# Moving the third output block's operand loads ahead of the gate loads, and giving the last four tiles four separate PSUM buffers

## The chip, the core and the metric

The kernel runs on one NeuronCore of a Trainium2 chip, as one launch. The metric is the device time of that launch in microseconds. Five engines work side by side, each through its own list of instructions in order: TensorE (PE, with the weight load shown apart as PEld), VectorE (DVE), ScalarE (ACT), GpSimd (POOL) and SyncE (SP, which here only starts DMAs). An instruction that waits for a semaphore holds up everything behind it on the same engine.

## The reference

For one sequence of S = 2048 tokens with D = 512 features, F = 1792 and 32 heads of 16:

```
xn = layernorm(x)
s  = softmax(q k^T / 4) v @ wo          with q, k, v = xn @ wqkv, 32 heads
g  = silu((silu(xn @ w_gate) * (xn @ w_up)) @ w_down)
out = x + s * g
```

Everything is float32. The kernel splits each operand of the large products into a high part, rounded to the matmul's reduced float32, and the low remainder, and adds three products (high by high, high by low, low by high).

## The kernel before

**Stages.** A prologue normalises x, transposes it and projects q, k and v, which go to DRAM. Then comes the main loop: 32 attention units (8 groups of four heads by 4 query blocks of 512 tokens), each of 8 steps. A step on TensorE is a fixed row of work: four score products (L809), the four products with v of the step before (`values`, L356) with ScalarE's exponentials (L811) between, four more score products, and then a share of side work.

**The side work** is a queue of generators, in order: four passes of the feed-forward net, a first part of the output projection of the last block, and `project_out(0)`, `project_out(1)`, `project_out(2)`, the output projections of query blocks 0, 1 and 2. `fill` takes products from it, `plan` has set how many per step. For the projections a share is one tile of 128 tokens: 12 pairs of products, each pair writing `bankx` and `banky` (`both`, L174). There are twelve such tiles; they take the last steps of unit 30 and all eight steps of unit 31. When a tile's last pair is done, VectorE empties the two banks into `y` (L328, L329), GpSimd multiplies by the gate and adds x (`store_out`, L313, L314) and the result is stored (L315). The next tile's first pair writes the same two banks, so TensorE waits for L328 and L329 of the tile before.

**Operands of an output block.** `load_out(b, c)` (L278, SP queue) brings part c of the attention output of block b from DRAM (`o_d`) into a raw slot, and `split_o` (L261 a cast, L262 a subtraction, VectorE) makes the high and low operand from it. Blocks 0 and 2 live in the tile `hh`, block 1 in `wd`; block 2 uses block 0's raw slots and operand slots again. A raw slot is free once block 0's split has read it, an operand slot once block 0's last product has. Part 3 of block 2 is not loaded: `finish(30)` makes it from the attention accumulator (L363 to L377, then a split).

**The order around it** is set by `out_steps`, called once per step behind the share. It issues a block's loads when a condition on the queue holds, appends its splits one step later, and hands VectorE at most two splits per step. `load_gates(t)` (L283 the gate, L284 x, SP queue) fetches what tile t needs on GpSimd. It reuses the slots of tile t - 4, so L283 waits for that tile's L313 and L284 for that tile's stored result. `after` is a list of things to do; `catch_up` runs it early in the next step.

**The end.** Behind the loop, block 3's output is finished by hand: `products(t, c)` (L856) for its four tiles into `outs[t]`, which are the four halves of the two score tiles; `normalise` for the last unit in two halves; then per tile `gated` (L863) and `stored` (L869 an addition, L870 the store).

Of the kernel before, what the change touches and what calls it, by code (L numbers as in the profile page):

```python
# [25 lines left out]
NB = 4  # L26
TB = S // NB
NT = TB // P
DT = D // P
# [21 lines left out]
def tile_block(ctx: ExitStack, tc: tile.TileContext, x, wqkv, wo, w_gate, w_up, w_down, out):  # L51
# [22 lines left out]
    banky = pone.tile([P, 512], F32, name="banky")  # L74
    banks = (bankx, banky)
    acc = [pone.tile([P, 512], F32, name=f"acc{i}") for i in range(2)]
# [77 lines left out]
    after = []  # L154

    def catch_up():
        while after:
            after.pop(0)()
# [13 lines left out]
    def both(lhs, rhs, start, stop):  # L172
        for bank, h in zip(banks, halves):
            mm(bank, lhs[h], rhs[h], start=start, stop=stop)  # L174
# [85 lines left out]
    def split_o(dst, src):  # L260
        dve.tensor_copy(dst[0], src)  # L261
        dve.tensor_sub(dst[1], src, dst[0].bitcast(F32))  # L262
# [11 lines left out]
    def load_out(b, c):  # L274
        whole = (hh, wd, hh)[b].rearrange("p f j t -> p (f j) t")
        parts_o[b, c] = whole[:, 2 * DT + c].bitcast(F32)
        lhs[b, c] = whole[:, 2 * c], whole[:, 2 * c + 1]
        sp.dma_start(parts_o[b, c], o_d[c, b])  # L278

    def load_gates(t):  # L280
        gt[t] = (hh, wd)[t % NT // 2].rearrange("p f j t -> p (f j) t")[:, 14 + t % 2].bitcast(F32)
        xr[t] = plain[t % NT]
        sp.dma_start(gt[t], g_d[rows[t]])  # L283
        sp.dma_start(xr[t], x[rows[t]])  # L284

    stage = {}
    ready = [0] * NB
    splits = []

    def out_steps():  # L290
        for b in range(NB - 1):
            if b not in stage and (len(queue) <= (NB, NB, 2)[b] if b != 1 else 0 in stage and now > stage[0]):
                for c in range(DT - 1):
                    load_out(b, c)
                stage[b] = now
            if b in stage and b < 2 and (b, 1) not in stage and now > (u0 + b) * steps:
                load_out(b, DT - 1)
                stage[b, 1] = now
            if b in stage and (b, 2) not in stage and now > stage[b]:
                splits.extend((b, c) for c in range(DT - 1))  # L300
                stage[b, 2] = now
                for t in range(0 if b else NT):
                    load_gates(t)
            if (b, 1) in stage and (b, 5) not in stage and now > stage[b, 1]:
                splits.insert(0 if not b else len(splits), (b, DT - 1))
                stage[b, 5] = now
        for _ in range(min(2, len(splits))):
            b, c = splits.pop(0)
            split_o(lhs[b, c], parts_o[b, c])
            ready[b] += 1  # L310

    def store_out(t, y):
        pool.tensor_mul(y, y, gt[t])  # L313
        pool.tensor_add(xr[t], y, xr[t])  # L314
        (pool if t < end - 1 else sp).dma_start(out[rows[t]], xr[t])  # L315

    def project_out(b, n=DT):
        catch_up()
        for j in range(NT if n == DT else EARLY):
            t = b * NT + j  # L320
            i = 0
            for c in range(n):
                for a, w in ((0, 0), (0, 1), (1, 0)):
                    both(lhs[b, c][a][:, j * P:(j + 1) * P], fx[:, w, c], i == 0, i == 3 * n - 1)
                    i += 1
                    if i == 3 * n and n == DT:
                        y = one.tile([P, D], F32, tag="th", name="y")
                        dve.tensor_scalar(y, bankx, 0.5, None, op0=ALU.mult)  # L328
                        dve.scalar_tensor_tensor(y, banky, 0.5, y, op0=ALU.mult, op1=ALU.add)  # L329
                        store_out(t, y)  # L330
                        if b + 2 < NB:
                            load_gates(t + NT)
                    elif i == 3 * n:
                        dve.tensor_copy(facc[:, j], bankx)
                        dve.tensor_add(facc[:, j], banky, facc[:, j])
                    yield 3 * n - i
# [50 lines left out]
    units = NG * NB  # L387
# [4 lines left out]

    queue = [[None, ffn(b), NF * 3 * (DC + NT)] for b in range(NB)]
    queue += [[None, project_out(NB - 1, DT - 1), EARLY * 3 * (DT - 1)]]
    queue += [[b, project_out(b), NT * 3 * DT] for b in range(NB - 1)]
    total = sum(q[2] for q in queue)
    given = 0

    now = -1
# [46 lines left out]
    with ExitStack() as pro:  # L446
# [294 lines left out]
        with tc.If(fast < 1):  # L741
            with tc.tile_pool(name="gen", bufs=1) as gen:
                for h in range(2):
                    pool.memset(qst[0][h * HALF:h * HALF + 2].bitcast(F32), 0.0)
                for g in range(NG):
                    for b in range(NB):
# [3 lines left out]
                        for j in range(NB):  # L750
                            load_k(g, j, j % 2)
                            for i in range(4 * NT):
                                h, t = divmod(i, NT)
# [28 lines left out]
    score = [spool.tile([P, 2, 512], F32, name=f"score{i}") for i in range(2)]  # L782
# [8 lines left out]
    now = 0  # L791
# [5 lines left out]
    for u in range(units):  # L797
        g, b = divmod(u, NB)
        q = qst[u % 2]
        for kp in range(steps):  # L800
            now = u * steps + kp
# [29 lines left out]
            if g + 1 < NG and (b == 0 and kp == 0 or b == NB - 1 and kp in (2, 4, 6)):  # L831
                load_k(g + 1, kp // 2)
                load_v(g + 1, kp // 2)
            out_steps()
            if now == (units - 1) * steps + 1:
                load_gate()
# [5 lines left out]
    assert not queue and not after and given == total  # L842
    hi = two.tile([P, 2, D], F32R, tag="guh", name="rh")[:, 0]
    lo = one.tile([P, D], F32R, tag="th", name="rl")
    outs = [i[:, n] for i in score for n in range(2)]
    half = TB // 2
    cols = [slice(n * half, (n + 1) * half) for n in range(2)]
    spare, *y = [ppool.tile([P, 2, TB], F32, tag="pr", name="y") for _ in range(3)]
# [13 lines left out]
    def gated(t):  # L862
        dve.scalar_tensor_tensor(y[t], outs[t], 0.5, gate[t], op0=ALU.mult, op1=ALU.mult)  # L863

    def stored(t, parts=1):
        n = D // parts
        for i in range(parts):
            w = slice(i * n, (i + 1) * n)
            dve.tensor_add(y[t][:, w], y[t][:, w], (facc[:, t] if t < EARLY else last[t])[:, w])  # L869
            (sp, nc.scalar)[(t + i) % 2].dma_start(out[rows[(NB - 1) * NT + t], w], y[t][:, w])  # L870
# [17 lines left out]
    for t in (2, 3):  # L888
        products(t, DT - 1)
        gated(t)  # L890
    stored(2)
    stored(3, 2)


_INS = ["A_x", "A_wqkv", "A_wo", "B_w_gate", "B_w_up", "B_w_down"]
# [21 lines left out]
```

## Time and profile before

| what | value |
|---|---|
| median of 3 runs | 1445.43 us (1444.51 to 1446.19) |
| the profiled execution's own time | 1447.62 us |
| its span, first to last instruction | 1445.8 us |
| granted TensorE clock, mean | 0.997 |
| TensorE busy | 1431.7 us (99%) |
| ScalarE busy | 1111.2 us (77%) |
| VectorE busy | 536.5 us (37%) |
| GpSimd busy | 89.1 us (6%) |

The profile comes from one execution. The time of that execution is its span and 1.8 us that lie outside it. Rows of the timeline read: start in us from the span's start, duration, engine, line, operation, output and input; in brackets how long the engine had been idle before and what ended the idle time. Rows of the waits read: who waited for whom, then us in total, how often, and the longest.

### The profile page before, as it was taken

What the parts mean: (1) busy time and instruction counts of PE and PEld (TensorE: products, weight loads), DVE (VectorE), ACT (ScalarE), POOL (GpSimd) and SP (SyncE); (2) the same over time, 40 slices, a digit from 0 to 9 for tenths busy, and PEclk for the clock granted to TensorE, in tenths of its full rate; (3) what the DMA queues carried; (4) which work ended last, traced back from release to release, by engine and by line L of the source; (5) the groups of instructions that cost most, each with busy time, mean ns of one, the idle gap of its engine ahead of it and who ended that gap; (6) DMA issues with size and microseconds to landing.
All of it is one profiled execution on the core that took longest, in us unless ns stands there. A gap on an engine that the chain in (4) does not pass through costs nothing.

```text
span 1445.8 us, 26814 instructions
## 1 busy us (share of the span) xinstructions
PE 1431.7 (99%) x11227; PEld 805.9 (56%) x11227; DVE 536.5 (37%) x900; ACT 1111.2 (77%) x1235; POOL 89.1 (6%) x103
## 2 busy tenths in 40 slices
PE   9999999999999999999999999999999999999988
PEld 7777655555555555555555555555555555555554
DVE  5543344213523443143334341234234421433735
ACT  6733688888888888788888888888888887888753
POOL 4200200000000000000000000000000000000244
PEclk9999999999999999999999999999999999999999
DMA  6778642032264330143534310333644211411553
GB/s 218 264 246 248 157 114 63 21 95 60 68 144 128 84 78 20 43 102 82 118 110 106 94 42 8 87 91 89 140 104 103 63 34 24 104 41 60 194 171 107
DMA packets 127524, 149.15 MB, mean 103 GB/s; under 512 B 12588, under 2 KB 79404, under 8 KB 126628
## 3 DMA queue, kind: packets, MB, share of 16 engines
q1 hardware_dynamic: 122196, 126.84, 34.0%
q0 software_dynamic: 4912, 20.12, 3.7%
q8 instruction: 91, 1.49, 0.4%
q10 hardware_dynamic: 288, 0.39, 0.1%
q14 instruction: 37, 0.30, 0.1%
HBM read 107.20 MB, written 40.11 MB: 102 GB/s over the span
## 4 chain that ended last, share of the span: by engine, by line
PE 96%; issue 1%; POOL 1%; DVE 1%; DMA 1%; ACT 0%; SPq 0%; POOLq 0%; DVEq 0%
PE acc L356 32%; PE bankx L174 30%; PE score L809 20%; PE ps L569 6%; PE banky L174 5%; PE ps L571 3%; PE acc L544 0%; POOL pair L314 0%; PE acc L493 0%; DMA hh<-o_d 0%; PE score L856 0%; PE ps L600 0%; DMA out_dram<-pair 0%; POOL y L313 0%; DMA out_dram<-y 0%
## 5 line engine op out<-in xcount | busy, mean ns | idle before, releaser
L811 ACT ACTIVATE pr<-score 128x1024 f32<-128x1024 f32 x1024 | 993.3, 1023 | 230.1 <-PE score L809 228.3
L356 PE MATMUL acc<-pr,vst 128*17 128x512 f32 x4096 | 489.2, 595 | 0.0
L809 PE MATMUL score<-qst,kst 50*128 50x512 f32 x2048 | 352.7, 421 | 0.9 <-ACT vt L631 0.9
L809 PEld LDWEIGHTS score<-qst,kst 50*128 50x128 f32 x2048 | 177.3, 184 | 264.7 <-ACT pr L811 228.8
L174 PE MATMUL bankx<-fx,guh 64*128 64x512 f32 x896 | 288.6, 392 | 0.0
L174 PE MATMUL banky<-fx,guh 64*128 64x512 f32 x896 | 288.4, 392 | 0.0
L356 PEld LDWEIGHTS acc<-pr,vst 128*17 128x17 f32 x4096 | 93.9, 96 | 234.7 <-issue 233.9
L204 DVE SCALAR_TENSOR_TENSOR ga<-th,bankx 128x512 f32<-128x512 f32 x56 | 38.5, 687 | 446.2 <-ACT th L203 446.2
L174 PEld LDWEIGHTS bankx<-fx,guh 64*128 64x128 f32 x896 | 165.8, 185 | 32.1 <-issue 0.3
L174 PE MATMUL bankx<-fx,gul 64*128 64x512 f32 x448 | 175.3, 391 | 0.0
L174 PE MATMUL banky<-fx,gul 64*128 64x512 f32 x448 | 175.3, 391 | 0.0
L174 PEld LDWEIGHTS banky<-fx,guh 64*128 64x128 f32 x896 | 165.8, 185 | 4.7
L174 PE MATMUL bankx<-wd,hh 64*128 64x512 f32 x672 | 166.7, 389 | 0.0
L174 PE MATMUL banky<-wd,hh 64*128 64x512 f32 x672 | 166.6, 388 | 0.0
L174 PEld LDWEIGHTS bankx<-wd,hh 64*128 64x128 f32 x672 | 124.0, 185 | 26.1
L174 PEld LDWEIGHTS banky<-wd,hh 64*128 64x128 f32 x672 | 124.0, 185 | 1.5
L174 PEld LDWEIGHTS bankx<-fx,gul 64*128 64x128 f32 x448 | 82.9, 185 | 17.2
L174 PEld LDWEIGHTS banky<-fx,gul 64*128 64x128 f32 x448 | 82.8, 185 | 2.1
L569 PE MATMUL ps<-xt,wh 128*128 128x512 f32 x256 | 80.7, 396 | 0.0
L222 DVE COPY facc<-bankx 128x512 f32<-128x512 f32 x16 | 11.1, 691 | 171.4 <-PE banky L174 171.4
L135 DVE TENSOR_TENSOR gul<-gur,guh 128x1024 fp32r<-128x1024 f32 x56 | 68.6, 1225 | 2.4 <-DVE guh L134 0.5
L569 PEld LDWEIGHTS ps<-xt,wh 128*128 128x128 f32 x256 | 47.8, 188 | 11.7 <-issue 0.4
(141 smaller groups left out, 1025.4 us busy)
## 6 DMA issues: line engine op xcount, KB each, us to landing
gur<-in_B_w_gate_dram SPq DMA_DIRECT2D x56, 256.0 KB
gur<-in_B_w_up_dram SPq DMA_DIRECT2D x56, 256.0 KB
wdr<-in_B_w_down_dram SPq DMA_DIRECT2D x56, 256.0 KB
kst<-k_d SPq DMA_DIRECT2D x192, 64.0 KB
qst<-q_d SPq DMA_DIRECT2D x192, 64.0 KB
fx<-xt_d SPq DMA_DIRECT2D x24, 512.0 KB
q_d<-parts SPq DMA_DIRECT2D x16, 512.0 KB
k_d<-parts SPq DMA_DIRECT2D x16, 512.0 KB
```

The source lines that it names most:

```text
L135: dve.tensor_sub(lo, raw, hi.bitcast(F32))
L174: mm(bank, lhs[h], rhs[h], start=start, stop=stop)
L204: dve.scalar_tensor_tensor(ga, th, 1.0, bankx, op0=ALU.add, op1=ALU.mult)
L222: dve.tensor_copy(facc[:, t], bankx)
L356: mm(a[h * 32:h * 32 + DH + 1], v[:, kt % CT, h * (DH + 1):(h + 1) * (DH + 1)], probs[2 * i + h // 2][:, h % 2], start=kt == 0, stop=kt == ...
L569: mm(ps, w, a[:, c], start=n == 0, stop=n == 3 * DT - 1)
L571: mm(ps, a[:, c, tokens], w, start=n == 0, stop=n == 3 * DT - 1)
L809: mm(score[j][:, h], k[r, j, kc * P:(kc + 1) * P], q[r, j], start=True, stop=True)
L811: exps.append(act(pr, score[j], AF.Exp, scale=0.25))
```

## The change

Three edits.

First, the condition under which block 2's loads are issued. Before, it was that at most two entries are left in the queue (block 0's projection is over). Now it is that all four splits of block 0 have been handed to VectorE. The splits of block 2 keep the old condition, now stated by itself, so they are handed out at the step where the queue gets that short, not one step behind it.

Second, `load_gates(t + 4)` is no longer called at the end of tile t's evacuation, but put on `after`, and so called in the next step.

Third, at the end `outs` are the first halves of the two score tiles, the accumulator that the last unit does not use, and `banky`: four separate tiles, where they were two halves each of two. With it, tile 2's addition and store stand ahead of tile 3's `gated`.

```diff
     def out_steps():
         for b in range(NB - 1):
-            if b not in stage and (len(queue) <= (NB, NB, 2)[b] if b != 1 else 0 in stage and now > stage[0]):
+            if b not in stage and (len(queue) <= NB, 0 in stage and now > stage.get(0, now), ready[0] == DT)[b]:
                 for c in range(DT - 1):
                     load_out(b, c)
                 stage[b] = now
...
-            if b in stage and (b, 2) not in stage and now > stage[b]:
+            if b in stage and (b, 2) not in stage and now > stage[b] and (b < 2 or len(queue) <= 2):
                 splits.extend((b, c) for c in range(DT - 1))
...
                         store_out(t, y)
                         if b + 2 < NB:
-                            load_gates(t + NT)
+                            after.append(partial(load_gates, t + NT))
...
-    outs = [i[:, n] for i in score for n in range(2)]
+    outs = (score[0][:, 0], score[1][:, 0], acc[units % 2], banky)
...
     for t in (2, 3):
         products(t, DT - 1)
         gated(t)
-    stored(2)
-    stored(3, 2)
+        stored(t, t - 1)
```

**SP's queue.** Here is the place of block 2's three loads (`hh<-o_d`, L278) in the SP queue. Before, the last four of the eight loads of gates and x for tiles 4 to 7 that stand ahead of them, then the three, then what follows:

```order
L283 DMA wd<-g_d 128x512
L284 DMA pair<-in_A_x_dram 128x512
L283 DMA wd<-g_d 128x512
L284 DMA pair<-in_A_x_dram 128x512
L278 DMA hh<-o_d 128x512 x3
L283 DMA hh<-g_d 128x512
```

And now, from block 1's four loads on:

```order
L278 DMA wd<-o_d 128x512 x4
L278 DMA hh<-o_d 128x512 x3
L283 DMA hh<-g_d 128x512
L284 DMA pair<-in_A_x_dram 128x512
L283 DMA hh<-g_d 128x512
L284 DMA pair<-in_A_x_dram 128x512
```

The three loads now stand directly behind block 1's four (`wd<-o_d`), ahead of the eight loads for tiles 4 to 7. Further down, the pair of loads for tile 9 now stands behind the eight of `load_gate` (L342, L343), not ahead of them.

**VectorE.** Here is what VectorE does between the evacuation of block 1's first tile and that of its second. Before, from that first evacuation to the second (the splits are L261 and L262 on `hh<-hh`, `finish(30)` is L363 to L262 on `hh<-o`):

```order
L329 SCALAR_TENSOR_TENSOR y<-banky,y 128x512
L261 CAST hh<-hh 128x512
L262 TENSOR_TENSOR hh<-hh 128x512
L261 CAST hh<-hh 128x512
L262 TENSOR_TENSOR hh<-hh 128x512
L363 STREAM_TRANSPOSE o_21035<-acc_85 128x512
L366 RECIPROCAL rl<-o_21035 128x16
L370 TENSOR_TENSOR on_9016<-o_21035,rl 128x16x16
L377 STREAM_TRANSPOSE o_21040<-on_9016 128x512
L261 CAST hh<-o_21040 128x512
L262 TENSOR_TENSOR hh<-o_21040,hh 128x512
L328 TENSOR_SCALAR y<-bankx 128x512
```

And now, from the evacuation of block 0's last tile (the first L329), through that of block 1's first tile (L328, L329), to the start of `finish(30)`:

```order
L329 SCALAR_TENSOR_TENSOR y<-banky,y 128x512
L261 CAST hh<-hh 128x512
L262 TENSOR_TENSOR hh<-hh 128x512
L261 CAST hh<-hh 128x512
L262 TENSOR_TENSOR hh<-hh 128x512
L328 TENSOR_SCALAR y<-bankx 128x512
L329 SCALAR_TENSOR_TENSOR y<-banky,y 128x512
L261 CAST hh<-hh 128x512
L262 TENSOR_TENSOR hh<-hh 128x512
L363 STREAM_TRANSPOSE o_21037<-acc_85 128x512
```

Two of block 2's splits moved up by one tile, and the third, which stood behind the second evacuation, now stands ahead of `finish(30)`. The rest of `finish(30)` and the second evacuation follow as before.

**TensorE at the end.** These are the last products, with what each waits for (`score_8985` and `score_8986` are the two score tiles, `acc_85` the free accumulator, `rh` and `rl` the operands from the last unit, `part` those that were there before). Before:

```order
L856 MATMUL score_8985<-fx,rl 128x512 [waits DVE_49]
L856 MATMUL score_8985<-fx,rh 128x512 [waits DVE_49]
L856 MATMUL score_8985<-fx,rh 128x512
L856 MATMUL score_8985<-fx,rl 128x512
L856 MATMUL score_8986<-fx,part 128x512 x6
L856 MATMUL score_8986<-fx,rh 128x512 [waits Activation_49]
L856 MATMUL score_8986<-fx,rh 128x512
L856 MATMUL score_8986<-fx,rl 128x512 [waits DVE_49]
L856 MATMUL score_8986<-fx,rh 128x512 [waits DVE_49]
L856 MATMUL score_8986<-fx,rh 128x512
L856 MATMUL score_8986<-fx,rl 128x512
```

And now:

```order
L856 MATMUL score_8985<-fx,rl 128x512 [waits DVE_49]
L856 MATMUL score_8986<-fx,rh 128x512 x2
L856 MATMUL score_8986<-fx,rl 128x512
L856 MATMUL banky<-fx,part 128x512 x6
L856 MATMUL acc_85<-fx,rh 128x512 [waits Activation_49]
L856 MATMUL acc_85<-fx,rh 128x512
L856 MATMUL acc_85<-fx,rl 128x512 [waits DVE_49]
L856 MATMUL banky<-fx,rh 128x512 x2
L856 MATMUL banky<-fx,rl 128x512
```

Two waits for VectorE are no longer there: the one ahead of tile 1's three products and the one ahead of tile 3's last three.

## The prediction

> **What bounds the kernel now.** I read the page first, for what the end of the program hangs on.
>
> ```profile
> span 1445.8 us, 26814 instructions
> PE 96%; issue 1%; POOL 1%; DVE 1%; DMA 1%; ACT 0%; SPq 0%; POOLq 0%; DVEq 0%
> ```
>
> The chain that ended last is TensorE for 96% of the span: the program takes as long as TensorE has products, plus the places where it stands. An edit that adds or removes no products can only touch those places. The chain leaves TensorE around 1380 to 1395 us and in the last 15 us, and these are the stretches that the change edits. So next I read the waits of 1376 to 1400 us, and three stretches of time.
>
> ```profile
> PE bankx L174 <- DVE y L328: 3.8, 1, 3.8
> DVE hh L261 <- DMA hh<-o_d: 4.7, 2, 3.5
> ...
> 1382.40:1388.20 5.80, 5.80 (x52) 3.31 (x48) 2.13 (x4) 3.88 (x4) 3.15 (x3) 1.00 0.66 232
> 1388.20:1400.50 12.30, 8.51 (x51) 4.89 (x48) 7.91 (x14) 3.88 (x4) 3.57 (x3) 0.72 0.32 105
> ...
> 1396.20:1398.20 2.00, 2.00 (x12) 1.63 (x10) 1.36 (x1) 0.00 (x0) 1.92 (x2) 0.50 0.07 20
> ```
>
> TensorE once stands 3.8 us for VectorE's L328, and VectorE ahead of that stands 4.7 us for the loads of block 2's raw parts. The stretches (engine columns, then granted clock, DMA share, GB/s) show a second cost: a normal step is all TensorE at clock 1.00; behind the stall the clock is 0.50. The timeline of TensorE gives both together:
>
> ```profile
> 1379.33 0.39 PE L174 MATMUL bankx<-fx,wd 64*128 64x512 f32 x1
> 1385.09 0.39 PE L174 MATMUL bankx<-fx,wd 64*128 64x512 f32 x1
> 1388.44 1.91 PE L356 MATMUL acc<-pr,vst 128*17 128x512 f32 x16
> 1394.80 0.79 PE L174 MATMUL bankx<-fx,wd 64*128 64x512 f32 x1 [3.79 <-DVE y L328]
> 1400.99 1.91 PE L356 MATMUL acc<-pr,vst 128*17 128x512 f32 x16
> 1406.77 1.91 PE L356 MATMUL acc<-pr,vst 128*17 128x512 f32 x16
> ```
>
> A step is 5.76 us (1379.33 to 1385.09) or 5.78 (1400.99 to 1406.77). The stalled one, between the two first L356 rows, is 12.55. The stall therefore costs 12.55 - 5.77 = **6.8 us**: 3.8 of standing and 3.0 of slow products behind it.
>
> Why was VectorE late? Its timeline, and below it SP's with SP's longest wait in 1376 to 1400 us:
>
> ```profile
> 1377.42 0.69 DVE L329 SCALAR_TENSOR_TENSOR y<-banky,y 128x512 f32<-128x512 f32 x1
> 1382.39 0.69 DVE L328 TENSOR_SCALAR y<-bankx 128x512 f32<-128x512 f32 x1 [4.28 <-PE banky L174]
> 1383.18 0.69 DVE L329 SCALAR_TENSOR_TENSOR y<-banky,y 128x512 f32<-128x512 f32 x1
> 1387.40 0.43 DVE L261 CAST hh<-hh 128x512 fp32r<-128x512 f32 x1 [3.53 <-DMA hh<-o_d]
> 1390.76 0.71 DVE L363 STREAM_TRANSPOSE o<-acc 128x512 f32<-128x512 f32 x1
> 1394.06 0.68 DVE L328 TENSOR_SCALAR y<-bankx 128x512 f32<-128x512 f32 x1
> 1394.85 0.69 DVE L329 SCALAR_TENSOR_TENSOR y<-banky,y 128x512 f32<-128x512 f32 x1
> ...
> 1350.61 2.47 SPq L278 DMA_DIRECT2D wd<-o_d  x4
> 1384.08 0.33 SPq L284 DMA_DIRECT2D pair<-in_A_x_dram  x1
> 1384.50 1.33 SPq L278 DMA_DIRECT2D hh<-o_d  x3
> ...
> SPq L284 <- DMA out_dram<-pair: 18.4, 4, 5.9
> ```
>
> The three loads are issued at 1384.50, directly behind a load of x that had to wait for a stored result. The first split starts 2.9 us later (1387.40). Two splits, then `finish(30)` (1390.76 to 1394.06, 3.30 us), then the evacuation that TensorE needs.
>
> **The change part by part.** *Loads earlier.* They now stand behind block 1's four loads, which SP issued from 1350.61 to 1353.08. They wait only for block 0's splits. This is the last of these, with the rows for what a split costs when GpSimd is at work, and GpSimd's:
>
> ```profile
> 1356.41 0.69 DVE L262 TENSOR_TENSOR hh<-hh 128x512 fp32r<-128x512 f32 x1
> 1366.94 1.66 DVE L262 TENSOR_TENSOR wd<-wd 128x512 fp32r<-128x512 f32 x1
> 1368.53 1.51 DVE L261 CAST wd<-wd 128x512 fp32r<-128x512 f32 x1
> ...
> 1366.67 1.39 POOL L313 TENSOR_TENSOR y<-y,hh 128x512 f32<-128x512 f32 x1 [1.83 <-DVE y L329]
> 1385.32 1.29 POOL L314 TENSOR_TENSOR pair<-y,pair 128x512 f32<-128x512 f32 x1
> ```
>
> So they can be issued by 1357.1. Before, they landed at latest 5.2 us after issue: the second split had its part, since `finish(30)` behind it began at 1390.76 and a split is 1.1 us. With that they have landed by 1363, fifteen microseconds ahead of the first split's new place. The 4.7 us wait of VectorE goes to nothing. The cover is these fifteen microseconds; without it the wait comes back at one for one.
>
> *Splits earlier.* The first two follow L329 at 1377.42. They add no work, but now fall beside GpSimd's L313 and L314, which start when L329 ends. There a split's subtraction lasts 1.66 us against 0.69, and a cast 1.51 against 0.43. Costed so: L329 0.60 to the next start, cast 0.45, subtraction 1.59 (1366.94 to 1368.53), slow cast 1.54, subtraction 0.61: VectorE is free at 1382.2, and the next evacuation is due at 1382.39. Even a microsecond late would be hidden: that bank pair is wanted at 1385.09.
>
> The third split follows L329 at 1383.18: 0.60 + 0.45 + 1.59, done at 1385.8. `finish(30)` takes its 3.30 us and ends at 1389.1, L328 starts then, L329 0.79 later, and ends at 1390.6. TensorE wants both banks at 1385.09 + 5.76 = 1390.85. It fits by a quarter of a microsecond. Bounds: nothing lost, or, if `finish(30)` is also held by GpSimd's L314 (it ended at 1386.6, and later if the split pushes it back; a held instruction costs 1.0 to 1.1 more, 1.66 - 0.69 or 1.51 - 0.43), L329 ends near 1391.7 and TensorE stands 0.9. I take 0, being nearer: most of `finish(30)` lies behind GpSimd's work. The Trainium skill speaks against this part of the change: GPSIMD Engine Reference, section "Key points", says that GpSimd shares its SBUF interfaces with VectorE and contends with instructions that have two SBUF inputs or use two ports. The 1.66 and 1.51 above agree; by that rule the product in `finish(30)` (L370, two SBUF inputs) is hit as well, which is the 0.9.
>
> So the stall's term is **-6.8**, between -5.9 and -6.8. Nothing stands behind it: ScalarE has 3.88 us of work in a 5.8 us step (the stretches above), and the next tiles' evacuations have no splits beside them.
>
> *Gates one step on.* The loads of gates and x wait for GpSimd of the tile four before, or for its stored result, wherever they stand in the list; the 18.4 us that SP stood for stored results are that. They are used four tiles later, four steps of 5.8 us. Tile 9's pair goes behind the eight loads of `load_gate`, at some 0.4 us of issue each (three in 1.33 us above). Cost 0; without that cover GpSimd, then the evacuation's `y`, would be late by what the load is late.
>
> *The end.* TensorE's and VectorE's rows from the products of tile 0 on:
>
> ```profile
> 1434.57 0.40 PE L856 MATMUL score<-fx,rl 128*128 128x512 f32 x1
> 1435.75 0.72 PE L856 MATMUL score<-fx,rh 128*128 128x512 f32 x2 [0.78 <-DVE y L863]
> 1436.55 1.56 PE L856 MATMUL score<-fx,part 128*128 128x512 f32 x6
> 1437.95 0.62 PE L856 MATMUL score<-fx,rh 128*128 128x512 f32 x2
> 1439.59 0.72 PE L856 MATMUL score<-fx,rh 128*128 128x512 f32 x2 [0.78 <-DVE y L863]
> ...
> 1435.62 0.41 DVE L860 TENSOR_TENSOR rl<-y,rh 128x256 fp32r<-128x256 f32 x1
> 1438.85 0.69 DVE L863 SCALAR_TENSOR_TENSOR y<-score,wd 128x512 f32<-128x512 f32 x1 [0.21 <-PE score L856]
> 1440.58 0.69 DVE L863 SCALAR_TENSOR_TENSOR y<-score,wd 128x512 f32<-128x512 f32 x1 [1.04 <-PE score L856]
> 1441.18 0.68 DVE L869 TENSOR_TENSOR y<-y,on 128x512 f32<-128x512 f32 x1
> 1441.78 0.75 DVE L869 TENSOR_TENSOR y<-y,last 128x256 f32<-128x256 f32 x2
> ...
> GB/s 15 15 0 0 0 0 0 0 0 0 0 97 369 190 0 0 0 0 0 0 0 0 276 384 374 277 0 0 0 20 0 51 389 346 341 184 0 0 0 0
> ```
>
> Twice TensorE stands until `gated` of the tile in the other half of the same score tile has read it. With separate tiles it goes on. A product follows the last by 0.233 us (six in 1436.55 to 1437.95). Tile 1's three start at 1434.80; then tile 3's six and tile 2's three; the last of these twelve starts 11 x 0.233 later and, 0.40 long, ends at 1437.8, tile 3's last at 1438.5. VectorE now sets the pace, at 0.60 a piece (1440.58, 1441.18, 1441.78): L860 ends at 1436.03, then `gated` 1, two additions, `gated` 2 at 1437.83, addition 2 at 1438.43, `gated` 3 at 1439.03, the last additions at 1439.63. Before, those began at 1441.78: **-2.15**. The new homes cost nothing: the free accumulator was read by `finish(30)` 38 us before, and `banky` is emptied by the queue's last L329 while nine products of tile 2 still stand ahead of its first one here. The bounds are TensorE's two pauses alone, 2 x 0.78 = 1.6, and the two pauses with their refilling (1434.80 to 1435.75, 1438.65 to 1439.59), 1.9, plus the moved addition's 0.60: 2.5.
>
> Behind the last addition come 3.3 us of store. Before, tile 2's store runs together with tile 3's; now it is out 1.2 us earlier. The GB/s row (40 slices of 0.4 us from 1430) shows the last bytes in five slices; tile 2's 262 kB, half of them, are 0.7 us at the row's 389. Between 0 and -0.7, I take **-0.3**.
>
> Sum: -6.8 - 2.15 - 0.3 = -9.25. Against the profiled execution (span 1445.8, and 1.8 outside it, 1447.62) that is 1438.4; it lies 2.2 above the median of the runs, so the runs give 1445.43 - 9.25 = **1436.2**.
>
> **The rivals.** *A: VectorE is late again at 1390.85*, because splits and `finish(30)` collide with GpSimd. For it: the quarter of a microsecond to spare, and 1.66 against 0.69. Against it: only the third split must collide. Price 0.9, so 1437.1; if the clock fell as behind the old stall, 3.0 more, not over 1440.1. The Trainium skill, TensorE: Matmul & The Clock Gate, section "Part 1: The HAM clock gate", has the array at half rate only after an idle window of about 3.4 us. The 0.50 behind 3.79 us agrees, and by it a pause of 0.9 costs 0.9.
>
> *B: the end is set by the stores.* Then the earlier additions meet a queue and only the stall goes: 1445.43 - 6.8 = 1438.6. For it: five of the last ten slices carry bytes at 341 to 389 GB/s. Against it: each of these stores is issued right behind its addition.
>
> *C: the loads don't land earlier*, held by a wait that the trace of before can't show at the new place. VectorE then stands with the first split ahead of the evacuation at 1382.39. With the old landing, L328 starts at 1390.76, TensorE gets bankx at 1391.5 instead of 1385.09: 6.4 idle and 3.0 at the slow clock, 2.6 more than now, less 2.45 at the end: 1445.6. From a landing 2.8 us later than the old one on it is over 0.2% slower, and 1449 at 3.4 later. Against it: block 0's splits are done by 1357.1.
>
> **How the numbers follow.** Forecast 0.72, A 0.15, B 0.09, C 0.04. The likeliest is 1436.2. Low: both bounds of the end, -2.5 and -0.7, and 0.9 for the runs' spread (1445.43 to 1444.51): 1434.5. High: B, and A with part of the slow clock, with the spread above: 1439.6. About 0.2% is what a measurement of this kernel can tell from no change, 1442.5 to 1448.3. The first three cases lie below, C within or above: faster 0.95, same 0.03, slower 0.02.
>
> **What would show it.** Right: the step from the old 1388.44 on is 5.8 us long and clock 1.00; SP's three loads stand before 1360; L261 never waits for them; the waits of L856 for L863 are gone, and the last L869 begins 9 us earlier. A shows as a wait of bankx or banky for L328 or L329 near 1391; B as the last addition earlier by 9 but the span by less than 8; C as L261 waiting for `hh<-o_d`. The forecast is wrong if another stall opens in the last eight steps, or if the three loads hold SP so long that the gates come late.

## The result

| | median | runs | ratio to before, 95% interval |
|---|---|---|---|
| before | 1446.01 us | 6, 1444.51 to 1447.56 | |
| the change | 1438.86 us | 6, 1437.99 to 1440.49 | 0.995 [0.9938, 0.9963] |

The change is faster by 7.15 us by the medians. By the two profiled executions (1447.62 and 1438.85) it is 8.8. The forecast time was 1436.2, from 9.25.

**The page and the steps.** From the page of the change: the span, and the chain of waits by engine.

```profile
span 1437.0 us, 26815 instructions
...
PE 98%; ACT 0%; DMA 0%; DVE 0%; issue 0%; SPq 0%; DVEq 0%
```

TensorE's share of the chain went from 96% to 98%. Its timeline and, below it, the step as a stretch (engine columns, granted clock, DMA share, GB/s) show that the stalled step is gone.

```profile
1388.69 1.91 PE L356 MATMUL acc<-pr,vst 128*17 128x512 f32 x16
1394.47 1.91 PE L356 MATMUL acc<-pr,vst 128*17 128x512 f32 x16
```

```profile
1388.69:1394.47 5.78, 5.78 (x51) 3.42 (x49) 2.39 (x5) 3.89 (x5) 3.09 (x3) 1.00 0.69 213
```

The step that took 12.55 us takes 5.78, all of it TensorE at clock 1.00. So 6.77 us went there. The step starts 0.25 later than before (1388.69 against 1388.44); that belongs to the 1388 us ahead of it, which vary from one execution to the next.

**SP and VectorE.** SP's queue and VectorE's timeline say why.

```profile
1349.92 3.78 SPq L278 DMA_DIRECT2D wd<-o_d  x4
1354.37 3.32 SPq L278 DMA_DIRECT2D hh<-o_d  x3
```

```profile
1378.73 1.66 DVE L262 TENSOR_TENSOR hh<-hh 128x512 fp32r<-128x512 f32 x1
1380.31 1.51 DVE L261 CAST hh<-hh 128x512 fp32r<-128x512 f32 x1
...
1384.50 1.65 DVE L262 TENSOR_TENSOR hh<-hh 128x512 fp32r<-128x512 f32 x1
1386.08 0.70 DVE L363 STREAM_TRANSPOSE o<-acc 128x512 f32<-128x512 f32 x1
...
1387.10 0.48 DVE L370 TENSOR_TENSOR on<-o,rl 128x256 f32<-128x256 f32 x1
...
1390.22 0.69 DVE L329 SCALAR_TENSOR_TENSOR y<-banky,y 128x512 f32<-128x512 f32 x1
```

The three loads are issued 30 us earlier (before: 1384.50), and no split waits for them. The subtraction and the cast that fall beside GpSimd's work last 1.66 and 1.51, to the hundredth what the rows of before gave for this collision. The evacuation ends at 1390.91. The first pair of a step is due 2.42 us after the start of the L356 row (1390.86 behind 1388.44 in a trace shown below), so TensorE wants the banks at 1388.69 + 2.42 = 1391.11. VectorE is 0.2 us ahead of it.

**The end.** TensorE's and VectorE's timelines from the products with the last operands on:

```profile
1428.26 0.62 PE L856 MATMUL score<-fx,rh 128*128 128x512 f32 x2
...
1431.04 0.64 PE L856 MATMUL banky<-fx,rh 128*128 128x512 f32 x2
```

```profile
1429.39 0.68 DVE L863 SCALAR_TENSOR_TENSOR y<-score,hh 128x512 f32<-128x512 f32 x1
1430.00 1.28 DVE L869 TENSOR_TENSOR y<-y,facc 128x512 f32<-128x512 f32 x2
1431.24 0.69 DVE L863 SCALAR_TENSOR_TENSOR y<-acc,wd 128x512 f32<-128x512 f32 x1
1431.96 0.69 DVE L869 TENSOR_TENSOR y<-y,on 128x512 f32<-128x512 f32 x1
1432.57 0.69 DVE L863 SCALAR_TENSOR_TENSOR y<-banky,wd 128x512 f32<-128x512 f32 x1
1433.29 0.76 DVE L869 TENSOR_TENSOR y<-y,last 128x256 f32<-128x256 f32 x2
```

TensorE no longer waits for `gated`, and VectorE goes from piece to piece without idle time. The last whole L356 row starts at 1422.82, so the last additions begin 1433.29 - 1422.82 = 10.47 us behind it; before it was 1441.78 - 1429.37 = 12.41. That is -1.94. From there to the end of the span it is 3.7 us, before 4.0. The three pieces and the offset, -6.8 + 0.25 - 1.94 - 0.3, make the 8.8 by which the spans differ.

### The profile page after: what moved, and what is told of

It is laid out like the page before. It is cut to its first block, busy times and chain, and to the rows that moved or that the text cites. A ratio compares the mean times of both kernels' runs of the same rounds, so it can differ in the third digit from the quotient of the medians.

```text
span 1437.0 us, 26815 instructions
## 1 busy us (share of the span) xinstructions
PE 1428.0 (99%) x11227; PEld 804.1 (56%) x11227; DVE 538.6 (37%) x900; ACT 1111.3 (77%) x1235; POOL 89.7 (6%) x103
## 4 chain that ended last, share of the span: by engine, by line
PE 98%; ACT 0%; DMA 0%; DVE 0%; issue 0%; SPq 0%; DVEq 0%
PE acc L356 33%; PE bankx L174 31%; PE score L809 20%; PE ps L569 6%; PE banky L174 4%; PE ps L571 3%; PE acc L544 0%; DMA wraw<-in_A_wqkv_dram 0%; PE ps L600 0%; DVE y L863 0%; PE acc L856 0%; PE bankx L576 0%; DVE y L869 0%; ACT vt L631 0%; ACT xt L549 0%
## 5 line engine op out<-in xcount | busy, mean ns | idle before, releaser
L356 PE MATMUL acc<-pr,vst 128*17 128x512 f32 x4096 | 489.2, 595 | 0.0
L356 PEld LDWEIGHTS acc<-pr,vst 128*17 128x17 f32 x4096 | 94.0, 96 | 234.7 <-issue 233.9
```

What stands on the lines that cost most here:

```text
L356: mm(a[h * 32:h * 32 + DH + 1], v[:, kt % CT, h * (DH + 1):(h + 1) * (DH + 1)], probs[2 * i + h // 2][:, h % 2], start=kt == 0, stop=kt == ...
```

## The experiments

The theory: TensorE's lost time near 1391 us goes because the loads no longer hold the splits, and the splits end before TensorE wants the banks; the end gains from separate tiles; the deferred gates do nothing. The rivals tested are a store-bound end, loads without effect of their own, and, for the price of what is left if VectorE is late, whether a pause of TensorE lowers the clock only when it is about 3.4 us long. Medians in one group are against the same runs of the kernel before: 1446.44 us (21 runs, 1444.16 to 1448.35) for the first four, 1446.19 (10 runs, 1445.11 to 1447.75) for the next four, 1445.83 (21 runs, 1443.66 to 1448.15) for the last four.

### The kernel before, again

> The kernel before, once more, for the clock and span of each of its executions. The profiled execution of before (1447.62 us, clock 0.997) stood 2.2 us over the median of its runs, and the measured gain (7.2 us by the medians) is 2 us less than the sum of the terms (9.25). Theory 1: the stall near 1391 costs 6.8 us in every execution, and the difference is scatter from elsewhere; then every execution shows about 0.997 and the times scatter without relation to the clock. Theory 2: the slow products behind the stall (3.0 us of the 6.8) come only in some executions, since the 3.8 us of standing are just about as long as it takes the clock to fall; then the clocks fall in two groups, 0.997 and 0.999 or more, and their times lie about 3 us apart.

Median 1446.15 us, ratio 1.0002 [0.9993, 1.0011]. The profiled execution took 1445.12, and its stall is not the one that the prediction costed. TensorE's rows (the wait in brackets) and three stretches of 3.4 us:

```profile
1387.68 1.91 PE L356 MATMUL acc<-pr,vst 128*17 128x512 f32 x16
...
1392.71 0.50 PE L174 MATMUL bankx<-fx,wd 64*128 64x512 f32 x1 [2.45 <-DVE y L328]
1393.51 0.49 PE L174 MATMUL banky<-fx,wd 64*128 64x512 f32 x1 [0.30 <-DVE y L329]
...
1398.50 1.91 PE L356 MATMUL acc<-pr,vst 128*17 128x512 f32 x16
```

```profile
1388.00:1391.40 3.40, 2.26 (x20) 0.53 (x12) 3.19 (x8) 2.84 (x4) 0.00 (x0) 1.00 0.37 113
1391.40:1394.80 3.40, 1.79 (x13) 1.26 (x15) 3.26 (x5) 0.60 (x1) 1.26 (x1) 1.00 0.14 51
1394.80:1398.20 3.40, 3.40 (x19) 2.53 (x15) 1.30 (x2) 0.00 (x0) 2.32 (x3) 0.50 0.34 95
```

The step took 10.82 us: the stall cost 5.05 here, not 6.8. And the clock went down two microseconds *after* the products had come back, and stayed down for 3.4. The two executions of the same kernel differ by 2.50 us; 1.73 of it is this step, the rest the 0.76 by which the L356 row before it starts earlier (1387.68 against 1388.44).

Neither theory stands as written. Of the 63 executions of before in this run and the three groups, six have a mean granted clock of 0.999 and are the fastest, 1443.66 to 1444.58 us; the others have 0.996 to 0.998 and take 1445.07 or more. So the clock does differ from execution to execution, but not in two groups 3 us apart.

### The change, again

> The changed kernel once more, beside its parts. No stall near 1391, so by both theories the clocks lie at 0.998 to 1.000; 1438.9 us by its first runs, 1436.2 by the forecast.

Median 1438.37 us (1437.79 to 1438.9, 5 runs), ratio 0.9945 [0.9932, 0.9959]: 8.07 less than before in this group. The eleven runs of the change, here and in the result, lie between 1437.79 and 1440.49, all but one below 1439; the 21 of before spread over 4.2 us. With the stall went most of the spread.

### The loads alone, and the tail alone

Loads alone: edits one and two, with the end of the kernel before.

```diff
-    outs = (score[0][:, 0], score[1][:, 0], acc[units % 2], banky)
+    outs = [i[:, n] for i in score for n in range(2)]
...
-        stored(t, t - 1)
+    stored(2)
+    stored(3, 2)
```

> The first two edits without the third (tail's tiles and order of stores as before). By the forecast's sum: 6.8 us under before, 2.45 over the change; the last L869 starts 12.4 us behind the first of the last L356, as before. Rival B (the end is set by the stores): within 0.5 us of the change.

Median 1440.74 us (5 runs), ratio 0.9963 [0.9949, 0.9976]: 5.7 under before. The end was kept, and its waits are back (VectorE's timeline):

```profile
1430.34 0.69 DVE L863 SCALAR_TENSOR_TENSOR y<-score,hh 128x512 f32<-128x512 f32 x1 [0.72 <-PE score L856]
...
1434.18 0.69 DVE L863 SCALAR_TENSOR_TENSOR y<-score,wd 128x512 f32<-128x512 f32 x1 [1.05 <-PE score L856]
```

The whole change lies 2.37 below this kernel, so that is what the third edit is worth.

Tail alone: the third edit put into the kernel before.

```diff
-    outs = [i[:, n] for i in score for n in range(2)]
+    outs = (score[0][:, 0], score[1][:, 0], acc[units % 2], banky)
...
-    stored(2)
-    stored(3, 2)
+        stored(t, t - 1)
```

> The third edit alone. By the forecast's sum: 2.45 us under before, with the stall near 1391 still 12.5 us for a step of 5.8 where the clock falls. Rival B: less than 0.5 us under before.

Median 1444.75 us (11 runs), ratio 0.9987 [0.9978, 0.9996]: 1.7 under before, with the other 6.4 still to gain. Together the parts alone make 5.7 + 1.7 = 7.4 of the whole 8.07; the intervals are 1.3 to 2 us to either side, so the parts add up as far as this can tell. An end that is set by its stores is refuted from both sides: the tail's gain shows with the loads and without them. In this trace the last additions begin 10.47 us behind the last whole L356 row, as in the change; in the loads alone and in both profiles of before it is 12.41 to 12.43. So the end's gain does not hang on the stall.

In this profiled execution the stall was again another one: TensorE's first pair behind it starts at 1394.20 and 1394.99, and the step from L356 to L356 is 12.20, 6.43 over a normal one.

### The gates, not deferred

```diff
-                            after.append(partial(load_gates, t + NT))
+                            load_gates(t + NT)
```

> The change without its second edit: the gates of tile t + 4 are asked for at once again. In SP's list one pair of loads (tile 4's) then stands ahead of block 2's three loads; in the change's trace that pair is issued at 1362.5 and 1366.9. Theory: the three loads go out near 1367.3, land by 1373, five microseconds ahead of the first split at 1378.3, so the time is that of the change within 0.5 us (1438.4). Rival: the second edit is needed, and without it the loads come late for the splits: then L261 waits for hh<-o_d and the time is 1 us or more over the change.

Median 1438.66 us (5 runs), ratio 0.9946 [0.9933, 0.996]: the same as the change. SP's queue has the loads at 1367.33 instead of 1354.37, behind one load of x, still some ten microseconds ahead of their splits. Beside the first edit the second is worth nothing.

### The gates deferred, the old conditions for block 2

```diff
-            if b not in stage and (len(queue) <= NB, 0 in stage and now > stage.get(0, now), ready[0] == DT)[b]:
+            if b not in stage and (len(queue) <= (NB, NB, 2)[b] if b != 1 else 0 in stage and now > stage[0]):
...
-            if b in stage and (b, 2) not in stage and now > stage[b] and (b < 2 or len(queue) <= 2):
+            if b in stage and (b, 2) not in stage and now > stage[b]:
```

> The change without its first edit (conditions of before for block 2's loads and splits), with the second and third. The three loads then stand ahead of tile 7's pair, and go out behind the load of x at 1380.2, near 1380.7; they land 2.9 and 5.2 us later at most, 1383.6 and 1385.9. Splits from 1384.05 beside GpSimd, the second done at 1388.2, finish(30) 3.4 us, L328 at 1391.6, L329 to 1393.1; TensorE wants both banks at 1391.1. Forecast: it stands 1.9 us, 1440.3; if the clock also falls behind so short a pause, up to 3.0 more.

Median 1440.15 us (5 runs), ratio 0.996 [0.9947, 0.9974]. The new end stays in this kernel. Without the first edit, the deferral moved the loads up by one of the waiting loads of x: they are issued at 1379.34 instead of 1384.50, and no split waits for a DMA. But the splits begin one step later than in the change, so that two of them stand ahead of `finish(30)`, not one. VectorE's rows of the second, and TensorE's rows:

```profile
1385.36 1.51 DVE L261 CAST hh<-hh 128x512 fp32r<-128x512 f32 x1
1386.90 0.69 DVE L262 TENSOR_TENSOR hh<-hh 128x512 fp32r<-128x512 f32 x1
1387.51 0.71 DVE L363 STREAM_TRANSPOSE o<-acc 128x512 f32<-128x512 f32 x1
```

```profile
1387.97 1.91 PE L356 MATMUL acc<-pr,vst 128*17 128x512 f32 x16
...
1391.56 0.49 PE L174 MATMUL bankx<-fx,wd 64*128 64x512 f32 x1 [1.01 <-DVE y L328]
1392.36 0.49 PE L174 MATMUL banky<-fx,wd 64*128 64x512 f32 x1 [0.30 <-DVE y L329]
...
1395.80 1.91 PE L356 MATMUL acc<-pr,vst 128*17 128x512 f32 x16
```

The step is 7.83, 2.06 too long. The second bank's first product starts 4.39 behind the L356 row, where 2.42 is normal: 1.97 late, which is the second split's 2.15 (1385.36 to 1387.51) less the margin of 0.2. That is the price, not the 1.01 in brackets. VectorE empties the banks one after the other, and TensorE needs both.

### The loads early, the splits one step later

```diff
-            if b in stage and (b, 2) not in stage and now > stage[b] and (b < 2 or len(queue) <= 2):
+            if b in stage and (b, 2) not in stage and now > stage[b] and (b < 2 or now > (units - NB + NB - 1) * steps - 1):
```

> The change with its loads early, but block 2's splits handed out one step later, as before. No wait for a load is left. VectorE: L329 at 1383.4, two splits beside GpSimd to 1388.2, finish(30) 3.4 us, L328 at 1391.6, L329 to 1393.1. Theory that the early loads alone are not the whole first edit: TensorE stands some 1.9 us at 1391.1, time 1440.3; a fall of the clock would add up to 3.0. Rival: the wait for the loads was all, and the time is that of the change.

Runs of 1439.73, 1440.1, 1441.84, 1442.19, 1442.2 and 1442.46 us; median 1442.02, ratio 0.9965 [0.9953, 0.9978]. So early loads alone are not the whole of it: against the kernel with the gates not deferred, in the same group, 3.4 us come back with the late splits by the median, and 1.1 and 1.4 in the two fastest runs. The pause in the profiled execution is the same as in the section above, yet the step is longer. TensorE's rows, and stretches of 3.4 us:

```profile
1388.43 1.91 PE L356 MATMUL acc<-pr,vst 128*17 128x512 f32 x16
...
1392.02 0.49 PE L174 MATMUL bankx<-fx,wd 64*128 64x512 f32 x1 [1.01 <-DVE y L328]
1392.82 0.49 PE L174 MATMUL banky<-fx,wd 64*128 64x512 f32 x1 [0.31 <-DVE y L329]
```

```profile
1390.10:1393.50 3.40, 2.09 (x15) 1.08 (x13) 3.19 (x7) 2.10 (x3) 0.65 (x1) 1.00 0.74 244
1393.50:1396.90 3.40, 3.40 (x20) 2.66 (x18) 1.29 (x1) 0.00 (x0) 2.93 (x3) 0.51 0.99 350
```

Both pauses make the second bank 1.97 late. The step here is 1397.82 - 1388.43 = 9.39, 3.62 too long, and not 2.06: the clock went to half 0.7 us after the second bank's first product and stayed there for 3.4 us.

### The additions on GpSimd

A version that might beat both: tiles 0 to 2 are added on GpSimd, since VectorE sets the pace of the end.

```diff
-            dve.tensor_add(y[t][:, w], ...)
+            (dve if t == 3 else pool).tensor_add(y[t][:, w], ...)
```

> The change with the last additions of tiles 0, 1 and 2 (L869) on GpSimd instead of VectorE. In the change's trace VectorE sets the pace behind the last product: gated 2 at 1431.24, addition 2 at 1431.96, gated 3 at 1432.57. Without addition 2 gated 3 starts when its products are done, 1431.95, and the end comes 0.6 us earlier: 1437.8, which runs hardly tell from 1438.4; the trace shows it as the last L869 0.6 us nearer to the last L356. Rival: GpSimd's addition of 1.3 us makes tile 2's store the last, and nothing is gained.

Median 1439.86 us (5 runs), ratio 0.9956 [0.9942, 0.9969]: 1.2 above the kernel with the gates not deferred, which has the change's end, in the same group. GpSimd's and VectorE's rows:

```profile
1431.81 1.26 POOL L869 TENSOR_TENSOR y<-y,on 128x512 f32<-128x512 f32 x1 [0.20 <-DVE y L863]
```

```profile
1432.41 1.27 DVE L869 TENSOR_TENSOR y<-y,last 128x256 f32<-128x256 f32 x2
```

The last additions begin 9.85 behind the last whole L356 row (at 1422.56), 0.6 earlier than in the change. But beside GpSimd's addition they last 1.27 instead of 0.76, which eats 0.5 of the 0.6, and tile 2's store follows GpSimd, whose addition ends 10.5 us behind that row where VectorE's ended 9.8 behind it. The span ends 1438.2 - 1433.68 = 4.5 us behind the last addition, where the change has 2.95. By the GB/s rows the bytes stop flowing at about 1435.4 in both; what holds the span's end here some 1.2 us longer behind the last bytes, the trace doesn't show.

### One, four and seven more transposes in `finish(30)`

VectorE is made late: the transpose of L377, 0.74 us apiece, is repeated for unit 30 with the same result.

```diff
-            dve.transpose(o2, on[b])
+            for _ in range(1 + 1 if u == units - 2 else 1): dve.transpose(o2, on[b])
```

> The change with one more transpose of 0.74 us in finish(30) (it writes the same o2 again): L329 of block 1's second tile ends near 1391.7 instead of 1390.9, where TensorE wants the bank at 1391.1. TensorE pauses 0.5 to 0.6 us. Theory A, the clock can fall behind a pause of any length of about a microsecond, by where it lies against something that runs by itself: most executions 1439.0, and a fall adds up to 2.5. Theory B, the clock falls only behind pauses of 3.4 us and more (the Trainium skill, TensorE: Matmul & The Clock Gate): all at 1439.0.

Median 1439.34 us (5 runs), ratio 0.9956 [0.9943, 0.997]. The second bank's first product starts at 1391.49, 3.03 behind the L356 row at 1388.46: 0.61 late. The step to 1394.94 is 6.48, 0.71 too long, at clock 1.00 throughout. So the margin is real: one more instruction of 0.74 us overruns it, and nothing else takes it up.

With `4 + 1` instead of `1 + 1`:

> Four more transposes: L328 ends near 1393.1, L329 near 1393.9, so TensorE stands some 2.0 us for bankx and 2.8 in all, without a DMA in the chain. Theory A: 1441.2 where the clock holds and 1443.5 to 1444 where it falls, in two groups or all in the second. Theory B: all at 1441.2, clock 1.00 behind the pause.

Runs of 1441.03, 1441.51 and 1441.64 us, seven from 1442.28 to 1443.2, and 1444.04; median 1442.85, ratio 0.9976 [0.9967, 0.9985]. TensorE's first pair behind the pause, and the stretches:

```profile
1392.14 0.50 PE L174 MATMUL bankx<-fx,wd 64*128 64x512 f32 x1 [1.89 <-DVE y L328]
1392.93 0.49 PE L174 MATMUL banky<-fx,wd 64*128 64x512 f32 x1 [0.30 <-DVE y L329]
```

```profile
1390.90:1394.30 3.40, 1.87 (x13) 1.33 (x15) 1.87 (x3) 1.09 (x2) 1.28 (x1) 1.00 1.00 348
1394.30:1397.60 3.30, 3.30 (x19) 2.46 (x15) 0.59 (x1) 0.00 (x0) 1.86 (x2) 0.50 1.03 372
```

The clock is at 0.50 behind a pause of 2.2 us in two pieces (1.89 and 0.30), so theory B is refuted. The three runs near 1441.4 (mean granted clock 0.999 to 1.000) and the eight from 1442.28 on (0.998) look like theory A's two groups, the second mostly faster than expected.

With `7 + 1`:

> Seven more transposes: TensorE stands 4.2 us for bankx and 5.0 in all. By both theories the clock falls every time: 1443.4 and 2.3 to 3.0 more, 1446 in one narrow group, where before (a stall of about this length whose start hangs on a DMA) scatters over 4 us.

Median 1445.81 us (11 runs, 1444.9 to 1446.28), ratio 1.0001 [0.9992, 1.001]: seven transposes give back all that the change brings. The pauses are as expected, and the runs are a narrow group, 1.4 us wide. But in the profiled execution the clock took 1.40 us and not 2.3 to 3.0. The stretches:

```profile
1388.50:1391.90 3.40, 2.39 (x20) 0.53 (x12) 3.23 (x6) 2.84 (x4) 0.00 (x0) 1.00 0.52 162
1391.90:1395.30 3.40, 0.28 (x1) 0.18 (x1) 3.19 (x6) 0.74 (x1) 0.00 (x0) 1.00 0.90 325
1395.30:1398.70 3.40, 3.19 (x15) 2.29 (x16) 0.46 (x1) 0.00 (x0) 2.54 (x2) 0.50 0.84 295
```

**All pauses in one table.** "Late" is the start of the second bank's first product behind the L356 row, less 2.42; "too long" is the step less 5.77; "half clock" is how long the clock was down.

| execution | late | too long | the rest | half clock |
|---|---|---|---|---|
| one transpose | 0.61 | 0.71 | 0.10 | none |
| gates deferred, old conditions | 1.97 | 2.06 | 0.09 | none |
| splits later | 1.97 | 3.62 | 1.65 | 3.4 |
| four transposes | 2.84 | 4.50 | 1.66 | 3.4 |
| before, again | 3.41 | 5.05 | 1.64 | 3.4 |
| tail alone | 4.23 | 6.43 | 2.20 | 6.8 |
| before | 4.74 | 6.78 | 2.04 | 6.8 |
| seven transposes | 5.08 | 6.48 | 1.40 | 3.4 |

What a pause costs is what it is late, plus half of the products' time at half clock: 3.4 / 2 = 1.7 where the whole 3.4 falls on products. It was down for 3.4 us or for twice that, never for another time. The kernel before, as first profiled, shows the double spell in three stretches, the first of them partly idle:

```profile
1389.60:1393.00 3.40, 1.42 (x12) 0.30 (x4) 3.14 (x7) 2.60 (x3) 0.00 (x0) 1.00 0.18 46
1393.00:1396.40 3.40, 1.59 (x5) 0.99 (x7) 3.23 (x6) 0.00 (x0) 0.77 (x1) 0.51 0.20 65
1396.40:1399.80 3.40, 3.40 (x18) 2.66 (x18) 1.17 (x1) 0.00 (x0) 2.81 (x3) 0.50 0.28 82
```

The reading that fits all eight: stretches of 3.4 us follow each other at a phase that differs from execution to execution, and one in which TensorE is busy for too little makes the next run at half clock. The stretches shown were cut at the fall, and backward from it: those ahead of half clock have TensorE busy for 0.28 to 2.09 us of 3.4 (here 1.42 and 1.59), those ahead of full clock 2.26, 2.39 and 3.40.

The phase can be read in every trace, since the clock falls once more behind the last products. In the six executions with a fall near 1391 that fall and the last one lie 13, 14 or 15 times 3.413 us apart, to 0.01 us (before: 1393.06 and 1444.26, 51.20 = 15 x 3.413). So a trace without a fall near 1391 can be cut backward from its end. With the gates deferred and the old conditions, the last fall is at 1436.42, and 13 times 3.413 ahead of it, at 1392.05, a boundary lies between the two pieces of the pause:

```profile
1388.64:1392.05 3.41, 2.40 (x17) 0.60 (x9) 3.20 (x6) 2.85 (x4) 0.00 (x0) 1.00 0.50 169
1392.05:1395.46 3.41, 3.11 (x27) 2.67 (x27) 2.25 (x3) 0.25 (x1) 2.99 (x2) 1.00 0.98 305
```

The pause of 1.3 us in two pieces that lay in one stretch with the late splits (TensorE busy for 2.09) is spread over two here (2.40 and 3.11), and the clock stays up. No run set the phase, but these two executions with the same lateness differ in it. A bound near 2.1 to 2.3 fits the stretches near 1391 only, so it is no rule: at the end of the change's trace, cut from its last fall at 1436.77, the stretch from 1429.95 to 1433.36 has TensorE busy for 1.96, and the next is at full clock. What is shown is that a pause far shorter than 3.4 us can lower the clock, with 1.6 us of price, and that the same pause need not.

The Trainium skill, TensorE: Matmul & The Clock Gate, section "Part 1: The HAM clock gate", has a free-running window of about 3.4 us; the spells of 3.4 and 6.8, and the whole numbers of 3.413 between the falls, agree. It puts the half rate behind at least one idle window, and here the traces differ: TensorE was busy for 2.09 of the 3.4 us ahead of a fall.

### Four tiles, but the old order of tile 2's addition and store

```diff
-        stored(t, t - 1)
+    stored(2)
+    stored(3, 2)
```

> The change with its four separate tiles, but tile 2's addition and store again behind tile 3's gated. This parts the third edit. Gated 3 then waits for its products (1431.95 in the change's trace) instead of following addition 2 (1432.57); addition 2 follows it, and the last additions start at most 0.1 us from where they are, 1433.3; tile 2's store goes out 0.6 us later and runs beside tile 3's, 0 to 0.4 us longer at the end. Forecast 1438.5, not to be told from the change; so the separate tiles are the term, and the moved addition nothing. Rival: the moved addition brings the 0.3 us at the stores, and the end of the span lies 0.3 or more behind the last L869 than in the change.

Median 1438.78 us (5 runs, 1438.38 to 1439.11), ratio 0.9953 [0.9939, 0.9967]: not to be told from the change. TensorE's normal step that gave the 2.42, and VectorE's end:

```profile
1388.44 1.91 PE L356 MATMUL acc<-pr,vst 128*17 128x512 f32 x16
...
1390.86 0.39 PE L174 MATMUL bankx<-fx,wd 64*128 64x512 f32 x1
```

```profile
1432.35 0.68 DVE L869 TENSOR_TENSOR y<-y,on 128x512 f32<-128x512 f32 x1
1432.95 0.76 DVE L869 TENSOR_TENSOR y<-y,last 128x256 f32<-128x256 f32 x2
```

The last additions begin 10.34 behind the last whole L356 row (1422.61), 0.13 sooner than with the moved addition, and the span ends 3.95 behind them instead of 3.7. So 0.25 of the 0.3 at the stores comes with the moved addition, nearly as the rival had it, but the move costs 0.13 ahead of it. The four tiles are the term; the order is worth 0.1 us in these two traces, less than the runs can tell.

## Why the prediction was right, and where it was off

**What bounds it: right.** TensorE's chain is 98% of the span after, 96% before. All of the gain lies in the two places named.

**The stall, -6.8: right for the execution it was read from, and mis-sized for the medians.** Between the two profiled executions the step lost 6.77. The step that failed is the one that carries the sum over: 1438.4 "lies 2.2 above the median of the runs, so the runs give 1445.43 - 9.25 = 1436.2". It took the 2.2 us for time that stays in both kernels. But the stall cost 6.8, 6.4 and 5.05 in the three executions with the old loads that were profiled, and between the first and the last of these it holds 1.73 of the 2.50 us. The end, as profiled (1.94 and 0.3), hardly differs from trace to trace, so the medians leave 4.9 (7.15 less 2.24) to 5.8 (8.07 less 2.24) for the stall: nearer its smallest size than its largest, though the execution at the median has no trace. What the change removes can't be subtracted in its largest size from a median that has a smaller one. A smaller part, 0.6, is that the median was one of three runs: six put it at 1446.01. The sum against its own execution, 1438.4, is 0.45 from the profiled run of the change, 1438.85; by the runs the loads alone are worth 5.7, and the ratio's interval [0.9949, 0.9976] reaches from 3.5 to 7.4.

**Its composition: off, the sum unharmed.** The prediction has 3.8 of standing and 3.0 of slow products. By the table it is 4.74 and 2.04: the row in brackets counts the wait for the first bank and not that for the second.

**Loads and splits: right.** The loads are issued from 1354.37 to 1357.69 (forecast: by 1357.1), L261 never waits, the slow subtraction and cast last 1.66 and 1.51, and the third split with `finish(30)` fits by 0.2 us where "a quarter" was written. That `finish(30)` was not held is in part luck, and not quite for the reason given, that most of it lies behind GpSimd's work. GpSimd's L314 lasted 1.62 us and ended at 1387.30, so L363, L366 and the first 0.2 us of L370 lay beside it. L363 and L366 took no longer than in before (0.70 and 0.25), and L370 took 0.06 more (0.48 instead of 0.42). What L370 would cost wholly beside GpSimd, where the prediction had 1.0 to 1.1, no run shows. The early loads without the early splits would have left 3.4 us by the median, as the run with late splits shows; the prediction counted both.

**The gates, 0: right** beside the first edit (1438.66 without the deferral). Alone it isn't nothing: the deferral and the tail with the old conditions make 1440.15, 6.0 under before, where the tail alone makes 1.7. It takes the last of the waiting loads of x from ahead of the three.

**The end, -2.15 and -0.3: right, a little less.** Profiled: -1.94 and -0.3; by medians 2.37 for both. The 0.2 is an instruction that reads what the one right ahead of it wrote: L863 to L869 of the same tile takes 0.72 from start to start (1431.24 to 1431.96, 1432.57 to 1433.29), and the sum had 0.60 everywhere. With the old order of tile 2's addition, where L863 of tile 3 is followed by L869 of tile 2, it is 0.61 (1431.74 to 1432.35).

**The rivals.** A: VectorE was not late. Its price stands where it is short (0.61 late cost 0.71). The clock's part was mis-sized: the prediction had "3.0 more" at most, and at 1.97 late it is 0 or 1.65, by the phase; at the 0.9 of rival A no run shows it. By the rule that the prediction cites from the Trainium skill, TensorE: Matmul & The Clock Gate, section "Part 1: The HAM clock gate", it would have been nothing. B: refuted by the loads alone and the tail alone. C: refuted by the SP row at 1354.37 and by L261, which never waits.

**The time.** 1438.86 lies inside the range of 1434.5 to 1439.6, but near its upper end, and not for the reason given there (the stores, or A): the median was reached from the wrong execution. That it still lies inside is partly luck, since the upper bound was made for other cases. Of the signs, the last L869 begins 8.5 us earlier (1441.78 to 1433.29) and not 9.

## What to carry to other kernels

A stall that hangs on a DMA's landing had another size in each of three executions here (6.8, 6.4, 5.05): cost such a stall against the execution that it was read from, or profile the kernel twice, and don't carry the full size to the median. Price a late engine by the last thing the waiting one needs (here the second bank), not by the wait that the profile puts in brackets. And a pause of TensorE of only some 1.3 us cost 1.65 us on top in one of two executions, so a margin of 0.2 us on the engine that feeds it is worth measuring, as one extra instruction did here.

## What the runs showed of the hardware that was not expected

The granted clock falls to 0.50 behind stretches in which TensorE was busy for as much as 2.09 of 3.4 us, up to two microseconds after the products have come back (1394.80 behind 1392.71 in the second profile of the kernel before), and it stays down for 3.4 or 6.8 us. Within an execution the falls lie a whole number of 3.413 us apart. The same kernel can have it in one execution and not in another: the runs with late splits lie at 1439.7 to 1440.1 (mean granted clock 0.999) and at 1441.8 to 1442.5 (0.998), some 2 us apart, which fits a pause of 1.97 without and with the 1.65.

VectorE's addition of two halves took 1.27 us beside GpSimd's addition and 0.76 alone, while the transpose of the accumulator showed no such hold (L363 0.70 at 1386.08 beside GpSimd, 0.71 before at 1390.76 without).
